# Moving the gate computation into attention, the row loads to the ScalarE queue, and narrowing the waits of late buffers

## The chip, the cores and the metric

The kernel runs on one core of one Trainium2 chip. The metric is the device time of one execution in microseconds, lower is better. Before the change the median of three runs is 730.36 us (727.07 to 731.42).

## What is computed

Attention within chunks of 64 positions, then a mixture of experts with one expert per token, chosen by cosine similarity. Everything is float32. Cut to what matters:

```python
# attention: q, k, v of shape (8, 8, 576, 64), in chunks of 64
scores = (q_c @ k_c.T) / sqrt(64)
attn = softmax(scores)                      # over the 64 keys of the chunk
x = (attn @ v_c)                            # -> (4608 tokens, 512)
# router and experts: 8 experts, w1 (8, 512, 1024), w2 (8, 1024, 512)
logits = (x / (|x| + 1e-6)) @ en.T / tau    # en: normalised expert embeddings
e = argmax(logits)
gate = 1 / (sum(exp(logits - max(logits))) + 1e-9)
out = gate * (relu(x @ w1[e]) @ w2[e])      # for each token with its own e
```

## The kernel before

**Two stages, one TensorE program.** Attention goes over 36 tiles `t` of 128 tokens. The expert stage goes over steps `j` (called blocks here): a block is 128 rows, 64 tokens of one expert in its lower half (`s` = 0) and 64 of another in its upper half (`s` = 1). One side works up from expert 0, the other down from expert 7. There are 37 blocks in this run; 36 of them are unrolled, and the last stands in a conditional section (`more`, L872). The schedule is manual: each engine runs its instructions in the order in which the Python code writes them.

**Attention** (L764 to L811). For a tile: transpose q and k (`turn_qk`), scores, subtract the maximum, Exp on ScalarE (`weights`), transpose, multiply with v (`values`), transpose x (`turn_x`), which also puts the sum of squares of each row beside it, then the eight logits. Four tiles make a group. For a group, `pick` (L514) finds the expert and `place` (L530) computes each token's row in a DRAM table `spots`, ordered by expert. `put` (L595) writes a tile's records there with an indirect DMA issued by GpSimd. A record is 512 values of x and 16 more: eight logits, the token number (`TOK`) and the sum of squares (`SQ`). Records wait in the ring `xr` of eight tiles; a slot is written again when its store has landed.

**Between the stages.** `groups`, `pad_places` and `places` (L646 on) turn the counts into tables: `src_row` (where a block's rows start), `eblk` (its expert) and `fresh` (whether the expert's weights have to be loaded). Padding records are stored last. Blocks 0, 1 and 2 hold rows of experts 0 and 7 alone, so they are loaded early (`load_early`), and the hidden layer of blocks 0 and 1 is computed in pieces inside attention (`early_parts`).

**Experts.** `load_x` (L144) reads two row numbers into registers and issues six DMAs, all on the SyncE queue: four pieces of x and two of the sixteen extra values (`spot`). `turn_xb` (L184) transposes the rows on VectorE. `hidden_part` (L213) does 64 matmuls for each half, then Relu on ScalarE and a transposition on VectorE. `result` (L242) does 64 matmuls, scales with the gate on ScalarE and writes out through an indirect DMA. `gates` (L196) computes the gate of a block: a square root on ScalarE, four VectorE operations, an Exp on ScalarE and two more VectorE operations. In the unrolled loop (L849) the hidden layer of block j+1 comes before the result of block j (of j-1 from the fourth round on), and the rows of block j+2 are transposed in the middle of hidden j+1.

**Weights.** Two buffers per layer and side. Buffer 0 is loaded in attention with experts 0 and 7. Buffer 1 is in the pool `late`, on bytes that attention used; block 4 (`LONE`) is the first to use it. `load_w` (L166) issues a load which moves nothing unless `fresh` is set. The first layer's weights of block 3 go out from ScalarE's queue, all later ones from SyncE's, in one order with the row loads. A weight load may go when the buffer's last reader is done: those of block j+2 wait for the matmuls of block j.

Of the kernel before, what the change touches and what calls it, by code (L numbers as in the profile page):

```python
# [9 lines left out]
FP32 = mybir.dt.float32  # L10
BF16 = mybir.dt.bfloat16
I32 = mybir.dt.int32
AF = mybir.ActivationFunctionType
ALU = mybir.AluOpType
AX = mybir.AxisListType
# [10 lines left out]
def kernel(  # L26
# [42 lines left out]

    MW = 16  # L70
    W = D + MW
    TOK, SQ = E, E + 1
    R = N + G * NE
    SPARE = E * R
    spots = nc.dram_tensor("spots", (SPARE + G, W), FP32, kind="Internal").ap()
# [47 lines left out]
            skip_runtime_bounds_check_because="a count of comparisons, less than this",  # L123
        )

    def load_rows(j, rows):

        xin[j] = xin_sb[j % XBUF]
        ins = []
        for s in range(2):  # L130
            for b in range(G // Q):
                c = s * (G // Q) + b
                ins.append(
                    nc.sync.dma_start(
                        out=xin[j][:, c * P : c * P + P],
                        in_=rows[s][Q * b : Q * b + Q, 0:D].rearrange("i (r d) -> r i d", d=P),
                    )
                )
            ins.append(
                nc.sync.dma_start(out=spot[G * s : G * s + G, j], in_=rows[s][:, D:W])  # L140
            )
        return ins

    def load_x(j):  # L144
        rows = []
        for s in range(2):
            row = number(src_row[G * s : G * s + 1, j - NE : j - NE + 1], SPARE, ENG.SP)
            rows.append(spots[ds(row, G), :])
        load_rows(j, rows)

    def first_rows(s, j, n):
        r0 = (0, E - 1)[s] * R + G * j
# [40 lines left out]
            )  # L193
        mo[j] = {"xT": xT}

    def gates(j):  # L196
        d = mo[j]
        lg = spot[:, j, 0:E]
        rn = bp.tile([P, 1], FP32, tag="rn", name="rn")
        lmax = bp.tile([P, 1], FP32, tag="lmax", name="lmax")  # L200
        sh = bp.tile([P, E], FP32, tag="sh", name="sh")
        gate = bp.tile([P, 1], FP32, tag="gate", name="gate", bufs=4)
        nc.scalar.activation(rn, spot[:, j, SQ : SQ + 1], AF.Sqrt)  # L203
        nc.vector.tensor_reduce(lmax, lg, axis=AX.X, op=ALU.max)
        nc.vector.tensor_scalar(rn, rn, 1e-6, None, ALU.add)
        nc.vector.reciprocal(rn, rn)
        nc.vector.tensor_scalar(sh, lg, lmax, rn, ALU.subtract, ALU.mult)  # L207
        nc.scalar.activation(sh, sh, AF.Exp, accum_out=gate)  # L208
        nc.vector.tensor_scalar(gate, gate, 1e-9, None, ALU.add)
        nc.vector.reciprocal(gate, gate)  # L210
        d["gate"] = gate

    def hidden_part(j, s, b, pool, tag, ps=None):  # L213


# [28 lines left out]
    def result(j, ps_y):  # L244
        d = mo.pop(j)
        ps = ps_y.tile([P, D], FP32, tag="y", name="y_ps")
        for c in range(KF):
            for r in range(P // Q):
                nc.tensor.matmul(  # L249
                    ps[Q * r : Q * r + Q],  # L250
                    lhsT=d["hT"][:, c, Q * r : Q * r + Q],
                    rhs=w2_sb[r // 2][buf_of(j)][:, c],
                    start=(c == 0),
                    stop=(c == KF - 1),
                )
        y = bp.tile([P, D], FP32, tag="y", name="y", bufs=3)
        nc.scalar.activation(y, ps, AF.Copy, scale=d["gate"])  # L257
        ins = nc.gpsimd.indirect_dma_start(  # L258
            out=out,
            out_offset=bass.IndirectOffsetOnAxis(ap=spot[:, j, TOK : TOK + 1].bitcast(I32), axis=0),  # L260
            in_=y,
            in_offset=None,
            bounds_check=N - 1,
            oob_is_err=False,
        )
        tc.declare_no_dep(ins.ins, group="rows", reason="blocks hold different tokens")
        tc.add_to_no_dep_group("rows", ins.ins)
# [8 lines left out]
    with (  # L276
# [26 lines left out]
        pref = one.tile([P, E], FP32, name="pref")  # L303
        e_base = one.tile([P, E], FP32, name="e_base")
        ones = one.tile([P, E], FP32, name="ones")
        part_i = one.tile([P, 1], I32, name="part_i")
        second = one.tile([P, 1], FP32, name="second")
        at = one.tile([P, 1], FP32, name="at")
# [18 lines left out]
        def constants():  # L327
# [5 lines left out]
            nc.gpsimd.memset(blank, 0.0)  # L333
            nc.gpsimd.memset(blank[:, D + TOK : D + TOK + 1].bitcast(I32), NO_ROW)
            nc.gpsimd.memset(ones, 1.0)
            nc.gpsimd.memset(before, 0.0)
            nc.gpsimd.memset(eqb_all[:, 0], 0.0)
            nc.gpsimd.memset(jump[:, 1], 1.0)
# [97 lines left out]
        def weights(t):  # L436
            a = st[t]["a"]
            nc.scalar.activation(a, a, AF.Exp, scale=scale)
# [75 lines left out]
        def pick(b):  # L514

            n, t = sizes[b], sum(sizes[:b])
            NE = [P, n, E]
            lg = copied.pop(b)
            lmax = wk.tile([P, RB], FP32, tag="lmax", name="lmax")[:, 0:n]
            sel = wk.tile([P, RB, E], FP32, tag="sel", name="sel")[:, 0:n]  # L520
            pm = wk.tile([P, RB], FP32, tag="pm", name="pm")[:, 0:n]
            nc.vector.tensor_reduce(lmax, lg, axis=AX.X, op=ALU.max)
            nc.vector.tensor_tensor(sel, lg, lmax.unsqueeze(2).to_broadcast(NE), ALU.is_equal)
            nc.vector.tensor_tensor(sel, sel, pref.unsqueeze(1).to_broadcast(NE), ALU.mult)
            nc.vector.tensor_reduce(pm, sel, axis=AX.X, op=ALU.max)
            nc.vector.tensor_tensor(
                eqb[:, t : t + n], sel, pm.unsqueeze(2).to_broadcast(NE), ALU.is_equal
            )

        def place(b):  # L530

# [232 lines left out]
        for t in range(-3, NT + 3):  # L764
# [29 lines left out]
                    load_v(b)  # L794
            if 0 <= t + 2 < NT:
                weights(t + 2)
            if t - 2 in ends:
                pick(ends[t - 2])
            if early_t <= t < early_t + NE:
# [14 lines left out]
        pad_places()  # L814
        put(len(to_put))
        places(0, 2)
        early_parts(NT + 3, 0)
        places(2, NST)
        nc.vector.tensor_copy(n_steps, mid[0:1])

    late_p = ctx.enter_context(tc.tile_pool(name="late", bufs=1))
    for s in range(2):
        w1_sb[s].append(late_p.tile([P, KD, F], FP32, name=f"w1_{s}1"))
    for s in range(2):
        w2_sb[s].append(late_p.tile([P, KF, D], FP32, name=f"w2_{s}1"))


    load_x(NE)
    load_x(NE + 1)
    load_w1(LONE)  # L830

    with (
        tc.tile_pool(name="ps_h", bufs=4, space=PSUM) as ps_h,
        tc.tile_pool(name="ps_y", bufs=2, space=PSUM) as ps_y,
    ):
        def hidden(j, turn=None):
            for s in range(2):
# [5 lines left out]
                    if turn + XBUF < NJ:  # L843
                        load_x(turn + XBUF)

        gates(0)

        LEAST = NT
        for j in range(LEAST + 1):  # L849
            if j == 0:  # L850
                gates(1)
            elif j + 1 < LEAST:
                hidden(j + 1, j + 2 if NE < j + 2 < LEAST else None)
                if NE <= next_of(j + 1) < NJ:
                    load_w1(next_of(j + 1))
            if j == 1:
                load_w2(LONE)
            if j + 2 < LEAST:
                if j + 2 <= NE:
                    turn_xb(j + 2)  # L860
                    load_x(j + 2 + XBUF)
                gates(j + 2)

            i = j if j < NE else j - 1
            if j != NE:
                result(i, ps_y)
                if NE <= next_of(i) < NJ:
                    load_w2(next_of(i))
# [3 lines left out]
        def more(j):  # L872
            with tc.If(steps > j - NE):
# [3 lines left out]
                hidden(j)  # L877
                if j + 2 < NJ:
                    load_w1(j + 2)
                gates(j)  # L880
                result(j, ps_y)
                if j + 2 < NJ:
                    load_w2(j + 2)
# [32 lines left out]
```

## Time and profile before

The profiled execution has a span of 735.0 us. The stages were read off the timeline of TensorE:

| stretch, us | what TensorE does |
|---|---|
| 0 to 206 | attention, and the hidden layer of blocks 0 and 1 between its tiles |
| 206 to 270 | blocks 0 to 5, with two holes |
| 270 to 709 | blocks in steady state, one step each 13.8 us |
| 709 to 726 | the last block, in the conditional section |
| 726 to 735 | the last store and the end of the program |

| group of instructions | busy, us | count |
|---|---|---|
| hidden matmuls, L229 | 279.9 | 4736 |
| result matmuls, L249 | 273.2 | 2368 |
| activation table loads, L203 and L208 | 47.5 each | 37 each |
| Relu, L238 | 44.2 | 74 |
| scaling of the result, L257 | 25.4 | 37 |
| transposition of rows, L188 | 43.1 | 74 |

A line of the timeline has the start, the duration, the engine, the line, the operation with what it writes and reads, and how many instructions were merged into it. In square brackets stands how long the engine was idle before it, and which engine, line or DMA ended that. For TensorE such a bracket is lost time; for the other engines idle time costs nothing by itself. `SPq` is the SyncE queue, where the duration is that of issuing a DMA and not of moving its data. A slice of the page is 18.4 us.

### The profile page before, as it was taken

The page shows a single profiled execution, that of the slowest core. Times are in us where ns is not written, and L with a number is a line of the kernel's source. Part 1 is how long each engine was busy: PE and PEld are TensorE (multiplying, and loading weights), DVE is VectorE, ACT ScalarE, POOL GpSimd, SP SyncE. Part 2 cuts the span into 40 slices and gives each one's busy share as a digit, 9 for nine tenths or more (in the row PEclk, how much of TensorE's full clock was granted, in tenths as well). Part 3 has the DMA queues.
Part 4 walks back from the last instruction along what each step waited for, and adds up shares of the span by engine and source line. Part 5 has one row for each costly group of instructions (what it writes and reads, how often), then busy time and mean ns, then how long its engine had stood idle before and what let it go on. Part 6 is the DMA issues. An engine that isn't in the chain of part 4 may idle for free. (4 is left out here: it accounts for less than half of the span.)

```text
span 735.0 us, 24771 instructions
## 1 busy us (share of the span) xinstructions
PE 685.2 (93%) x10327; PEld 399.4 (54%) x10327; DVE 264.0 (36%) x729; ACT 286.3 (39%) x518; POOL 123.9 (17%) x188
## 2 busy tenths in 40 slices
PE   6589999998969979999999999998999999999994
PEld 5579898986624434444444444443454554554441
DVE  4347787887272321321321321321122222222100
ACT  4346666664243333343343343342334334334112
POOL 7114454434131001001001001000000000000010
PEclk9779999998889999999999999999999999999998
DMA  9989999989727811116784416789751264411340
GB/s 197 191 193 212 250 246 253 242 198 327 285 82 275 276 29 56 35 42 207 254 324 170 162 44 222 275 314 330 270 180 43 72 234 159 147 45 44 132 169 16
DMA packets 139445, 132.36 MB, mean 180 GB/s; under 512 B 85332, under 2 KB 105812, under 8 KB 139328
## 3 DMA queue, kind: packets, MB, share of 16 engines
q1 hardware_dynamic: 130192, 101.95, 47.4%
q0 software_dynamic: 9104, 28.75, 12.7%
q8 instruction: 83, 1.36, 0.8%
q14 instruction: 34, 0.28, 0.1%
q10 hardware_dynamic: 32, 0.02, 0.0%
HBM read 349.52 MB, written 21.46 MB: 505 GB/s over the span
## 5 line engine op out<-in xcount | busy, mean ns | idle before, releaser
L229 PE MATMUL h_ps<-w,xbT 128*32 128x256 f32 x4736 | 279.9, 385 | 14.3 <-DMA w<-in_moe_w_dram 8.0
L249 PE MATMUL y_ps<-w,hT 128*32 128x512 f32 x2368 | 273.2, 592 | 4.6 <-DMA w<-in_moe_w_dram 3.2
L229 PEld LDWEIGHTS h_ps<-w,xbT 128*32 128x32 f32 x4736 | 167.5, 112 | 124.6 <-issue 32.8
L249 PEld LDWEIGHTS y_ps<-w,hT 128*32 128x32 f32 x2368 | 86.9, 110 | 161.3 <-issue 149.2
L239 DVE STREAM_TRANSPOSE hT<-h 128x512 f32<-128x512 f32 x74 | 52.6, 711 | 299.1 <-ACT h L238 299.1
L238 ACT ACTIVATE h<-h_ps 128x512 f32<-128x512 f32 x74 | 44.2, 597 | 217.7 <-PE h_ps L229 213.9
L258 POOL DMA_INDIRECT out_dram<-y,spot x37 | 36.3, 980 | 479.6 <-ACT y L257 426.7
L257 ACT ACTIVATE y<-y_ps,gate 128x512 f32<-128x512 f32 x37 | 25.4, 687 | 102.3 <-PE y_ps L249 102.3
L208 ACT ACT_TABLE_LOAD x37 | 47.5, 1283 | 24.6 <-DVE sh L207 24.5
L203 ACT ACT_TABLE_LOAD x37 | 47.5, 1283 | 2.8 <-DMA w<-in_moe_w_dram 2.2
L598 POOL DMA_INDIRECT spots<-xr,dest x36 | 37.1, 1031 | 48.9 <-DVE dest L563 16.1
L379 POOL DMA_DIRECT2D qx<-in_q_dram x40 | 35.1, 884 | 60.0 <-PE tr L402 59.5
L489 ACT COPY xT<-tr 128x512 f32<-128x512 f32 x36 | 21.1, 586 | 59.2 <-PE tr L487 59.2
L188 DVE STREAM_TRANSPOSE xbT<-xin 128x256 f32<-128x256 f32 x74 | 43.1, 621 | 0.1
L402 PE MATMUL tr<-ident,kx 128*128 128x128 f32 x144 | 24.6, 299 | 14.1 <-DMA kx<-in_k_dram 14.0
L499 PEld LDWEIGHTS rt_ps<-enT,xT 128*128 128x128 f32 x288 | 37.1, 202 | 1.0 <-issue 0.8
L499 PE MATMUL rt_ps<-enT,xT 128*128 128x8 f32 x288 | 36.6, 254 | 0.0
L407 DVE COPY qxT<-tr 128x512 f32<-128x512 f32 x36 | 24.8, 688 | 21.3 <-PE tr L402 20.5
L426 DVE TENSOR_REDUCE mx<-sc 128x8 f32<-128x512 f32 x36 | 24.9, 691 | 17.4 <-PE sc L418 16.4
L458 PE MATMUL pv<-v,aT 64*64 64x65 f32 x1152 | 27.5, 233 | 2.6 <-issue 2.2
L418 PE MATMUL sc<-kxT,qxT 64*64 64x64 f32 x1152 | 27.3, 235 | 0.4 <-issue 0.4
L458 PEld LDWEIGHTS pv<-v,aT 64*64 64x64 f32 x1152 | 21.9, 141 | 9.5 <-issue 9.0
(137 smaller groups left out, 446.4 us busy)
## 6 DMA issues: line engine op xcount, KB each, us to landing
w<-in_moe_w_dram SPq DMA_DIRECT2D x146, 2048.0 KB
xin<-spots SPq DMA_DIRECT2D x160, 64.0 KB
kx<-in_k_dram SPq DMA_DIRECT2D x32, 256.0 KB
qx<-in_q_dram POOLq DMA_DIRECT2D x32, 256.0 KB, 5.5
v<-in_v_dram SPq DMA_DIRECT2D x56, 144.0 KB
w<-in_moe_w_dram ACTq DMA_DIRECT2D x2, 2048.0 KB
spot<-spots SPq DMA_DIRECT2D x80, 4.0 KB
qx<-in_q_dram POOLq DMA_DIRECT2D x8, 128.0 KB, 6.7
```

The source lines that it names most:

```text
L188: nc.vector.transpose(xT[:, :, cols].rearrange("p c (b i) -> p b c i", i=Q), t[:, s * (D // 2) : (s + 1) * (D // 2)].rearrange("p (b i c) ...
L203: nc.scalar.activation(rn, spot[:, j, SQ : SQ + 1], AF.Sqrt)
L208: nc.scalar.activation(sh, sh, AF.Exp, accum_out=gate)
L229: nc.tensor.matmul(ps[Q * r : Q * r + Q, b].rearrange("p (k i) -> p k i", i=Q), lhsT=d["xT"][:, c, t0 : t0 + Q], rhs=w[:, c, r], start=(c ...
L238: nc.scalar.activation(h, ps, AF.Relu)
L239: nc.vector.transpose(hT[:, :, G * s : G * s + G].rearrange("p k (b i) -> p b k i", i=Q), h.rearrange("p b (k i) -> p b k i", i=Q),)
L249: nc.tensor.matmul(ps[Q * r : Q * r + Q], lhsT=d["hT"][:, c, Q * r : Q * r + Q], rhs=w2_sb[r // 2][buf_of(j)][:, c], start=(c == 0), stop= ...
L258: ins = nc.gpsimd.indirect_dma_start(out=out, out_offset=bass.IndirectOffsetOnAxis(ap=spot[:, j, TOK : TOK + 1].bitcast(I32), axis=0), in_ ...
L379: eng.dma_start(out=x[done : done + n], in_=src[b, :, s : s + n, :].rearrange("h p d -> p h d"),)
L458: nc.tensor.matmul(pv[CH * c : CH * c + CH, par, i], lhsT=d["aT"][r0 : r0 + CH, i, CH * c : CH * c + CH], rhs=v_t[b][r0 : r0 + CH, i, cb, ...
L499: nc.tensor.matmul(rt_ps[:, batch_of[t][0] % 2, batch_of[t][1]], lhsT=d["xT"][:, c], rhs=enT[:, c], start=(c == 0), stop=(c == KD - 1),)
L598: ins = nc.gpsimd.indirect_dma_start(out=spots, out_offset=bass.IndirectOffsetOnAxis(ap=at, axis=0), in_=m, in_offset=None, bounds_check=S ...
```

## The change

It has four parts. First, the gate is computed in attention, for a group of four tiles at once, and written into the record (field `GATE`), so that it arrives with the rows. The square root becomes a power of 0.5 on GpSimd, which spares ScalarE its change of tables. Second, the row loads of all blocks from 3 on are issued by ScalarE, so that only weights are left on SyncE. Third, the pools made after attention (`late`, `ps_h`, `ps_y`) wait only for those earlier users whose bytes they take over, and not for all users of the pools that lay there. Fourth, the order at the start of the expert stage: the rows of block 2 are transposed before the long tables of `places`, the weights of block 4 are asked for first, and the rows of block 5 are loaded ahead of the loop.

```diff
-    TOK, SQ = E, E + 1
+    TOK, SQ, GATE = E, E + 1, E + 2
...
-    def load_rows(j, rows):
+    def load_rows(j, rows, eng=nc.sync):
...
-                    nc.sync.dma_start(
+                    eng.dma_start(
...
-            row = number(src_row[G * s : G * s + 1, j - NE : j - NE + 1], SPARE, ENG.SP)
+            row = number(src_row[G * s : G * s + 1, j - NE : j - NE + 1], SPARE, ENG.Activation)
             rows.append(spots[ds(row, G), :])
-        load_rows(j, rows)
+        load_rows(j, rows, nc.scalar)
...
-    def gates(j):
-        d = mo[j]
-        lg = spot[:, j, 0:E]
...
-        nc.scalar.activation(rn, spot[:, j, SQ : SQ + 1], AF.Sqrt)
-        nc.vector.tensor_reduce(lmax, lg, axis=AX.X, op=ALU.max)
-        nc.vector.tensor_scalar(rn, rn, 1e-6, None, ALU.add)
-        nc.vector.reciprocal(rn, rn)
-        nc.vector.tensor_scalar(sh, lg, lmax, rn, ALU.subtract, ALU.mult)
-        nc.scalar.activation(sh, sh, AF.Exp, accum_out=gate)
-        nc.vector.tensor_scalar(gate, gate, 1e-9, None, ALU.add)
-        nc.vector.reciprocal(gate, gate)
-        d["gate"] = gate
...
-        nc.scalar.activation(y, ps, AF.Copy, scale=d["gate"])
+        nc.scalar.activation(y, ps, AF.Copy, scale=spot[:, j, GATE : GATE + 1])
...
+            sq = xr[:, t % NX : t % NX + n, D + SQ]
+            nc.gpsimd.tensor_tensor(rn, sq, halves[:, 0:n], ALU.pow)
+            nc.vector.tensor_scalar(rn, rn, 1e-6, None, ALU.add)
+            nc.vector.reciprocal(rn, rn)
+            nc.vector.tensor_tensor(sh, lg, lmax.unsqueeze(2).to_broadcast(NE), ALU.subtract)
+            nc.vector.tensor_tensor(sh, sh, rn.unsqueeze(2).to_broadcast(NE), ALU.mult)
...
+        def gates(b):
...
+            nc.scalar.activation(sh, sh, AF.Exp)
+            gs = wk.tile([P, RB], FP32, tag="gs", name="gs")[:, 0:n]
+            nc.vector.tensor_reduce(gs, sh, axis=AX.X, op=ALU.add)
+            nc.vector.tensor_scalar(gs, gs, 1e-9, None, ALU.add)
+            nc.vector.reciprocal(xr[:, t % NX : t % NX + n, D + GATE], gs)
...
                 weights(t + 2)
+            if t - 3 in ends:
+                gates(ends[t - 3])
             if t - 2 in ends:
                 pick(ends[t - 2])
...
         places(0, 2)
+        turn_xb(2)
         early_parts(NT + 3, 0)
         places(2, NST)
...
-    late_p = ctx.enter_context(tc.tile_pool(name="late", bufs=1))
+    late_p = ctx.enter_context(tc.tile_pool(name="late", bufs=1, reuse_waits="tile"))
...
+    load_w1(LONE)
     load_x(NE)
     load_x(NE + 1)
-    load_w1(LONE)
+    load_x(NE + 2)
...
-        tc.tile_pool(name="ps_h", bufs=4, space=PSUM) as ps_h,
-        tc.tile_pool(name="ps_y", bufs=2, space=PSUM) as ps_y,
+        tc.tile_pool(name="ps_h", bufs=4, space=PSUM, reuse_waits="tile") as ps_h,
+        tc.tile_pool(name="ps_y", bufs=2, space=PSUM, reuse_waits="tile") as ps_y,
...
-        gates(0)
...
-            if j == 0:
-                gates(1)
-            elif j + 1 < LEAST:
+            if 1 < j + 1 < LEAST:
                 hidden(j + 1, j + 2 if NE < j + 2 < LEAST else None)
...
-            if j + 2 < LEAST:
-                if j + 2 <= NE:
-                    turn_xb(j + 2)
-                    load_x(j + 2 + XBUF)
-                gates(j + 2)
+            if j + 2 == NE:
+                turn_xb(NE)
+                load_x(NE + XBUF)
```

## The prediction

> **What bounds the kernel now.** I read the page first. TensorE is busy 93% of the span, and the slices show it short of full in the attention part and again near slices 11 to 14 and 27. The chain that ended last holds only the final store, so I took the waits from the timeline of TensorE.
>
> ```profile
> PE 685.2 (93%) x10327; PEld 399.4 (54%) x10327; DVE 264.0 (36%) x729; ACT 286.3 (39%) x518; POOL 123.9 (17%) x188
> PE   6589999998969979999999999998999999999994
> L203 ACT ACT_TABLE_LOAD x37 | 47.5, 1283 | 2.8 <-DMA w<-in_moe_w_dram 2.2
> ```
>
> Next, the timeline of TensorE from 195 us (start, us, engine, line, what, count, idle before):
>
> ```profile
> 205.78 7.05 PE L249 MATMUL y_ps<-w,hT 128*32 128x512 f32 x64
> 218.49 9.50 PE L229 MATMUL h_ps<-w,xbT 128*32 128x256 f32 x128 [5.66 <-DVE xbT L188]
> 227.80 7.06 PE L249 MATMUL y_ps<-w,hT 128*32 128x512 f32 x64
> 234.66 7.09 PE L229 MATMUL h_ps<-w,xbT 128*32 128x256 f32 x128
> ...
> 261.24 8.61 PE L229 MATMUL h_ps<-w,xbT 128*32 128x256 f32 x128 [5.71 <-DMA w<-in_moe_w_dram]
> ...
> 508.02 7.06 PE L249 MATMUL y_ps<-w,hT 128*32 128x512 f32 x60 [3.17 <-DMA w<-in_moe_w_dram]
> 516.43 7.11 PE L229 MATMUL h_ps<-w,xbT 128*32 128x256 f32 x128 [1.35 <-DMA w<-in_moe_w_dram]
> ```
>
> A step is 128 matmuls of L229 (6.9 us from start to start) and 64 of L249 (6.9), 13.8 us. From 269.9 to 504.8 and from 516.5 to 709.2 TensorE is busy in every microsecond (the windows give 234.90 of 234.90 and 192.70 of 192.70), so work taken off other engines there is worth nothing. Only the holes can be won: 5.66, 5.71, 3.17 and 1.35 us, and the two slow stretches after the long ones: 9.50 and 8.61 instead of 7.09, 2.4 and 1.5 us. Sum 19.8 us.
>
> Who ends these holes? VectorE and ScalarE at the first, the SyncE queue at the second:
>
> ```profile
> 215.82 1.28 ACT L208 ACT_TABLE_LOAD   x1
> 217.63 0.16 DVE L210 RECIPROCAL gate<-gate 128x1 f32<-128x1 f32 x1
> 217.72 1.14 DVE L188 STREAM_TRANSPOSE xbT<-xin 128x256 f32<-128x256 f32 x2
> 225.39 1.95 SPq L169 DMA_DIRECT2D w<-in_moe_w_dram  x2
> 230.20 4.42 SPq L140 DMA_DIRECT2D spot<-spots  x1
> 261.01 3.95 SPq L169 DMA_DIRECT2D w<-in_moe_w_dram  x4
> ```
>
> Block 2's rows were long in SBUF; their transposition (217.72) stood on VectorE behind the gates of blocks 0 and 1, which waited for ScalarE's table loads. The second hole ends 0.23 us after SyncE issued the weights of block 5 (261.01): no expert changed, so nothing had to move, but the issue stood behind row loads slowed by the two weight loads of 225.39. At 487.53 likewise: that block's weights could go when its matmuls ended (476.4), but SyncE was issuing rows from 475.03 to 486.05.
>
> [...] 5.66 us idle, then granted clock 0.74 over 9.3 us; after 3.17 us none.
>
> **The change part by part.** *Gates out of the expert steps.* 74 table loads (95 us of ScalarE), and per block two activations and six VectorE operations go. In the full stretches this is hidden by TensorE. It counts at the first hole: with gates(0), gates(1) gone and turn_xb(2) before places(2,...), the transposition follows the `fresh` row at 208.6, before result(0) ends at 212.83. First hole and slow stretch go: block 2 starts at 212.8 instead of 218.5.
>
> *Gates into attention.* Per group of four tiles VectorE gets seven small operations of 0.15 to 0.20 us (rows L522 to L526), about 1.4 us; ScalarE one Exp of 0.2; GpSimd one power, unpriced by page or trace. Its nearest row, a 128x8 tensor_tensor, took 0.20 us; I allow 0.2 to 1.5. It is on the path where iota waits for stores (178.10) just when VectorE wants it. VectorE has no idle from 160.5 to 162.2 in such a group; x is written until 165.92 and transposed from 166.44, a slack of 0.5 us against 0.85 added ahead. So about 0.4 us in late groups, none in early ones (`before` takes 0.22 us there, 0.6 later). Also the first store of a group waits for its gate, some 2 us later; its slot is rewritten 7.3 us after issue (147.78 to 155.11) with 6.0 us to land, so 0.7 us may show. Lower end 0, upper end 8 groups of 1.4 = 11 us. I take 2.5.
>
> *Rows on the ScalarE queue.* The cost of one load there is not in the trace. On SyncE it is 4.4 us for six issues (213.43 to 217.85) and 5.9 from load to load; two weight issues of ScalarE took 1.43 us (229.30), 0.7 each; six of them and about 1 us for the two registers make 5.2. In a steady step ScalarE then has 5.2 + 1.9 (two Relu of 0.60, one y of 0.69) = 7.1 of 13.8 us. Relu of half 1 waits behind the issues, until about 12.6 us after the step's start; its hT is wanted 20.8 us after. Hidden. But at the start three loads (3, 4, 5) stand ahead of y(0) and Relu of block 2. They can't begin before the padding stores have landed (213.4): 213.4 + 3 x 5.2 - 0.8 = 228.2. Then y 0.69, two Relu, two hT of 0.71, half an xbT 0.6: block 3 starts at 231.8. TensorE ends result(1) at 226.6 and idles 5.2 us, then pays 2.4 us of slow clock: block 3 ends at 241.3, before 241.75. Nearly all of the first win is given back.
>
> *Weights alone on SyncE.* Block 4's weights go out near 210 instead of 225, its second half when load 4 has begun (about 222), and are there by 230, wanted at 248. Block 5's null load goes when block 3 ends (241.3). So the second hole (5.71) and its slow 1.5 go: result(3) starts at 241.3 + 3 x 6.9 = 262.0 instead of 269.66, 7.7 us earlier. At 476.4 the new weights go 11 us earlier; they and the second layer's are 8 MB, 21 us at the 373 to 401 GB/s that the windows from 490 to 505 show, wanted 27 us after the first issue; so both holes there (4.5 us) should close. In the built program a row load waits for the transfer eight before it on either queue; near a change of experts that is a weight of the step before, some 10 us old: a few us, inside the Relu's slack.
>
> *Waits by bytes.* Late buffers wait only for users of their own bytes. This concerns the second weight buffers, which lie on attention's tiles, and the PSUM banks. The expert number comes only at 208.4, so it lets the first half go near 210, counted above; no hole of before names a PSUM user of another bank, so the banks bring nothing.
>
> *Tail.* Block 36 has load 39 ahead of its Relus on ScalarE: 711.0 + 0.7 + 4.4 = 716.1, when Relu of half 1 is due at 717.2. 0 to 1 us; I take 0.3.
>
> Sum: +2.5 - 7.7 - 4.5 + 0.3 = -9.4; 730.4 - 9.4 = 721.0.
>
> **The rivals.** *Issue on ScalarE is slow while weights move* (chance 0.25). For: a row issue took 0.57 us at the median but up to 4.55 on SyncE, 4.42 at 230.20. Load 5 meets the weights of block 4; then block 3 starts 4.4 us later, half of the 4.5 stays, the tail takes 1: +2.5 - 3.3 - 2.2 + 1 = -2.0, 728. Against: those shared one queue with the weights. *VectorE becomes the bound of attention* (0.12): the full 11 us, with the slow issue and no gain at 508: +11 - 3.3 + 1 = +8.7, 739, slower. For: VectorE's full rows around each group. Against: it idles 0.76 us in each other tile. *ScalarE's loads don't delay block 3* (0.11): hole of 5.2 and slow 2.4 go too: 713.4. For: only if issues are near 0.3 us. Against: every issue shown is 0.5 or more.
>
> **How the numbers follow.** The forecast has 0.52. Its own unknowns (attention 0 to 5, the three loads 2 us either way) spread it over 716 to 725. The range is 713 to 733: it takes in the slow issue with its spread, and leaves out most of the VectorE case. One per cent is 7.3 us: faster needs under 723.1, most of the forecast (0.42), the last rival, and a little of the slow issue: 0.58. Within 1%: 0.30. Slower: 0.12.
>
> **What would show it.** Right: block 2's matmuls follow result(0) with no gap; a gap of about 5 us moves in front of block 3, ended by the transposition; none before block 5; none near 505; no table load after attention. Attention's last L229 ends 0 to 5 us later than 205.9. Wrong: Relu rows on ScalarE that wait so long that TensorE gaps recur in steps with weight traffic; row issues of over 1 us on ScalarE; or attention longer by over 5 us.

## The result and the profile after

The changed kernel takes 750.37 us at the median (747.58 to 752.08, four runs) against 729.5 us (727.07 to 731.42) for the kernel before: a ratio of 1.0284, 95% interval 1.0239 to 1.033. It is slower by almost 3%, where the prediction had it faster by 1.3%. A second measurement of both on another chip gave 752.55 (two runs) and 729.17 us, 1.0305 (1.02 to 1.0411). Medians and ratios count executions in the faster of two states; it matters for one run alone, the first with only the gates moved, where five of twelve executions, the traced one among them, were slower.

The page of the changed kernel first, the engine totals and TensorE's slices (here 18.7 us each):

```profile
PE 684.5 (92%) x10327; PEld 391.5 (52%) x10327; DVE 235.1 (31%) x570; ACT 174.1 (23%) x342; POOL 133.0 (18%) x198
PE   5589998999992999999989999987999999999994
```

ScalarE has lost 112 us of work and VectorE 29, as meant; no table load is left in the expert stage. TensorE does the same work, and, after attention, has a deep notch in slice 13 and shallow ones in slices 21, 27 and 28. Its timeline after attention (start, us, engine, line, operation, count, idle before) shows them; L212 is the hidden layer, L232 the result:

```profile
204.75 7.05 PE L232 MATMUL y_ps<-w,hT 128*32 128x512 f32 x64
211.62 7.09 PE L212 MATMUL h_ps<-w,xbT 128*32 128x256 f32 x128
218.53 7.05 PE L232 MATMUL y_ps<-w,hT 128*32 128x512 f32 x64
239.14 8.77 PE L212 MATMUL h_ps<-w,xbT 128*32 128x256 f32 x128 [13.56 <-DVE xbT L188]
...
254.60 13.99 PE L212 MATMUL h_ps<-w,xbT 128*32 128x256 f32 x256
268.42 7.04 PE L232 MATMUL y_ps<-w,hT 128*32 128x512 f32 x64
...
383.19 7.96 PE L232 MATMUL y_ps<-w,hT 128*32 128x512 f32 x58 [3.11 <-DMA w<-in_moe_w_dram]
...
498.71 8.66 PE L232 MATMUL y_ps<-w,hT 128*32 128x512 f32 x64 [2.73 <-DMA w<-in_moe_w_dram]
...
520.86 9.09 PE L232 MATMUL y_ps<-w,hT 128*32 128x512 f32 x58 [4.74 <-DMA w<-in_moe_w_dram]
```

The hole ahead of block 2 is gone (211.62 follows the result of block 0 directly), and so is the one ahead of block 5 (254.60 runs through two hidden layers). In their place stands one of 13.56 us ahead of block 3. In the steady part, where before had holes only near 510, there are now holes at 383, 499 and 521, each ended by a weight transfer and each followed by a stretch at the slow clock (granted at 0.52 from 383 to 386, at 0.50 from 499 to 501 and from 521 to 523).

What did the weights wait for? The waits of the SyncE queue from 205 us to the end (engine, line, what it waited for: us in total, times, longest), where L169 issues the weights:

```profile
SPq L169 <- DMA xin<-spots: 259.2, 59, 16.1
SPq L169 <- DMA w<-in_moe_w_dram: 87.7, 12, 10.5
SPq L169 <- PE y_ps L232: 25.3, 7, 7.7
```

SyncE issues nothing but weights now, and it spends 259 us waiting for the landing of row loads, which ScalarE issues. Before, its weights waited for TensorE to be done with a buffer, and for no row load:

```profile
SPq L134 <- DVE xbT L188: 86.7, 25, 4.7
SPq L169 <- PE y_ps L249: 28.6, 21, 5.6
```

No weight needs a row. The wait comes from the completion semaphores, as the trace's records of the transfers show, which name the semaphore that each one raises and those that it waits for. From 205 us on, SyncE (142) and ScalarE (224) issue 366 transfers. They raise the same eight semaphores, and 364 of them wait for the very one that they raise. GpSimd's 45 transfers raise eight others. A step of the changed kernel issues six row transfers and four weight loads; the last transfer on a weight's semaphore was a row load 73 times and another weight 70 times, and a row load had a weight ahead of it 70 times. The trace of before has eight semaphores for its 366 transfers as well, taken in turn (in 345 of 358 cases the same one comes again with the eighth transfer after it), but there 364 of the transfers stand in one queue, in that order, and the wait shows little (1.7 us of weights for weights). The Relus on ScalarE show the other direction, again from the table of waits:

```profile
ACT h L221 <- DMA spot<-spots: 90.6, 14, 9.2
ACT h L221 <- DMA w<-in_moe_w_dram: 67.4, 10, 11.2
ACT h L221 <- DMA xin<-spots: 57.4, 9, 8.3
```

A Relu needs neither. The row loads that stand ahead of it on ScalarE wait, and some of them for weights (67.4 us, in ten waits). So weights wait for rows, and rows for weights and for ScalarE's own work. In the issues of weights by SyncE from 490 to 506 us of the changed kernel (three windows of the timeline) the effect is seen: they go out one at a time until 500, just when the experts change. The two long waits in this stretch were ended by other weights (12.5 us together); ahead of the hole at 383 SyncE had waited 7.0 us for a row load.

```profile
491.99 0.09 SPq L169 DMA_DIRECT2D w<-in_moe_w_dram  x1
498.70 0.38 SPq L169 DMA_DIRECT2D w<-in_moe_w_dram  x1
500.29 2.85 SPq L169 DMA_DIRECT2D w<-in_moe_w_dram  x3
```

The kernel before had sent its four together:

```profile
487.53 4.06 SPq L169 DMA_DIRECT2D w<-in_moe_w_dram  x4
```

### The profile page after: what moved, and what is told of

Its sections match the earlier page's. It is cut to its first block, busy times and chain, and to the rows that moved or that the text cites. A ratio compares the mean times of both kernels' runs of the same rounds, so it can differ in the third digit from the quotient of the medians.

```text
span 748.1 us, 24343 instructions
## 1 busy us (share of the span) xinstructions
PE 684.5 (92%) x10327; PEld 391.5 (52%) x10327; DVE 235.1 (31%) x570; ACT 174.1 (23%) x342; POOL 133.0 (18%) x198
## 3 DMA queue, kind: packets, MB, share of 16 engines
q0 software_dynamic: 9104, 28.75, 12.5%
## 5 line engine op out<-in xcount | busy, mean ns | idle before, releaser
L212 PE MATMUL h_ps<-w,xbT 128*32 128x256 f32 x4736 | 283.3, 382 | 16.1 <-DVE xbT L188 13.6
L232 PE MATMUL y_ps<-w,hT 128*32 128x512 f32 x2368 | 283.9, 602 | 11.7 <-DMA w<-in_moe_w_dram 10.6
L212 PEld LDWEIGHTS h_ps<-w,xbT 128*32 128x32 f32 x4736 | 164.1, 110 | 128.5 <-issue 17.6
L232 PEld LDWEIGHTS y_ps<-w,hT 128*32 128x32 f32 x2368 | 89.3, 112 | 173.4 <-issue 157.9
L240 ACT ACTIVATE y<-y_ps,spot 128x512 f32<-128x512 f32 x37 | 25.4, 687 | 163.7 <-PE y_ps L232 114.4
L387 PEld LDWEIGHTS tr<-ident,kx 128*128 128x128 f32 x144 | 17.6, 149 | 22.5 <-issue 16.7
L387 PE MATMUL tr<-ident,qx 128*128 128x128 f32 x144 | 23.5, 290 | 2.4 <-DMA qx<-in_q_dram 2.4
```

Source lines behind the costliest of these rows:

```text
L212: nc.tensor.matmul(ps[Q * r : Q * r + Q, b].rearrange("p (k i) -> p k i", i=Q), lhsT=d["xT"][:, c, t0 : t0 + Q], rhs=w[:, c, r], start=(c ...
L232: nc.tensor.matmul(ps[Q * r : Q * r + Q], lhsT=d["hT"][:, c, Q * r : Q * r + Q], rhs=w2_sb[r // 2][buf_of(j)][:, c], start=(c == 0), stop= ...
L387: nc.tensor.transpose(ps[:, i], a[:, i * P : i * P + P], ident)
```

## The experiments

Runs of one comparison share a chip and its runs of the kernel before; ratios are to those. Theory 1 is the reading above. Its rival, theory 2: the loss lies in the gates in attention, the narrower waits or the new order.

### Rows moved between the queues, and each main part alone

*The changed kernel with rows back on SyncE* (here and below, the engine that reads the row numbers into registers is changed along with it):

```diff
-        load_rows(j, rows, nc.scalar)
+        load_rows(j, rows, nc.sync)
```

> The changed kernel with the row loads of blocks 3 to 36 back on the SyncE queue; gates in attention, order and waits by bytes stay. Theory 1 (rows on ScalarE are the cause: they stand behind Relus there, and weights on SyncE then wait for rows through the completion semaphores that both queues take in turn): no hole at 383, at most the 4.5 us of before near 510, block 3 not 13.6 us late. About 750 - 14 (weight holes) - up to 13 at the entry = 723 to 736. Theory 2 (gates in attention, waits by bytes or the new order cost the time): stays at 745 to 752.

Measured: 739.58 us, ratio 1.0095 (1.006 to 1.013). The hole at 383 is gone and one of 4.19 us is left at 511, like before's. The total misses the range, for two reasons: the hole ahead of block 5 came back at 7.97 us, and on this chip the last matmuls of block 1 crawled for 7 us (called the crawl below; last section).

*The same rows on GpSimd* (`nc.gpsimd` in that line):

> The changed kernel with the same row loads issued by GpSimd, which has its own completion semaphores and almost no work in the expert stage. Theory 1: the holes near 383, 499 and 521 go (some 14 us), and the hole ahead of block 3 shrinks from 13.6 us to at most 4, as no Relu stands behind a load: 715 to 728. Theory 2: 745 to 752, as on SyncE. If issuing through GpSimd is itself slow (several us for each of six), holes in steady steps of 13.8 us would return, each ended by the transposition of rows: over 735.

Measured: 727.42 us, ratio 0.9921 (0.9891 to 0.9951), although its trace has the crawl as well. After it TensorE has no hole of over half a microsecond until the conditional block at 709, and no weight on SyncE waits for a row. Again on a chip without the crawl:

> The changed kernel with rows on GpSimd once more, beside the two others. Its first run (727) had no hole in the steady part, but 7 us of single matmuls near 212 and a slow clock after it, some 9 us, which the kernel before and the changed one did not show on their chip. Without that: 715 to 720; if it belongs to this kernel: 725 to 730.

Measured: 714.15 us (709.42 to 717.76), ratio 0.980 (0.9757 to 0.9843). This is just under its range, and the fastest median of the study. TensorE's timeline of that run shows the entry:

```profile
220.46 7.12 PE L212 MATMUL h_ps<-w,xbT 128*32 128x256 f32 x128 [0.40 <-DVE xbT L188]
...
234.25 14.00 PE L212 MATMUL h_ps<-w,xbT 128*32 128x256 f32 x256
```

Block 3 waits 0.40 us in place of 13.56, and blocks 4 and 5 follow without a gap; up to 690 us no hole is longer. Nothing but the issuing engine of the rows differs from the changed kernel, and 36 us lie between the two medians. They are of two chips, but the ratios, 0.980 and 1.0284, lie as far apart.

*The kernel before with rows on ScalarE, nothing else:*

> The kernel before with one edit: the row loads of blocks 3 to 36 are issued by ScalarE. Theory 1: slower by 10 to 20 us (740 to 750), with holes in the steps with weight traffic near 383, 500 and 520 that are ended by DMA w, and waits of SyncE's weight issues (L169) for row loads of over 100 us in all. Theory 2: the same as before, 727 to 733, as the cost lies in the other parts.

Measured: 760.86 us, ratio 1.0375 (1.0308 to 1.0442), above the range. The holes of the steady part are there, some 12 us later than in the changed kernel, since this chip has the crawl and a hole of 18.08 us opens at the entry (here ahead of block 2). SyncE's waits name the same cause:

```profile
394.91 8.33 PE L249 MATMUL y_ps<-w,hT 128*32 128x512 f32 x58 [2.43 <-DMA w<-in_moe_w_dram]
...
532.81 9.40 PE L249 MATMUL y_ps<-w,hT 128*32 128x512 f32 x58 [4.33 <-DMA w<-in_moe_w_dram]
```

```profile
SPq L169 <- DMA xin<-spots: 230.4, 56, 13.6
```

So this one part alone costs about as much as the whole change, or more (the intervals of the two ratios overlap a little). Theory 2 is out as the main cause.

*The kernel before with the gates in attention, nothing else* (the diff of the gates as in the change, rows on SyncE, old order and waits), twice:

> The kernel before with one edit: the gates are computed in attention and travel in the records; rows stay on SyncE, the old order and the old waits stay. Theory 1: attention costs nothing, the first hole (5.66 us and 2.4 us of slow clock) shrinks as no table load stands ahead of block 2's transposition, the weight holes of before stay: 721 to 730. Theory 2: the gates cost time in attention, 735 to 750.

> The kernel before with the gates in attention and nothing else, once more, as its first run had the same 7 us of single matmuls. If that is not of this kernel: block 2 starts 0 to 6 us earlier than in before, the hole ahead of block 5 stays: 722 to 730. If it is: 734 to 740.

Measured: 736.81 us and ratio 1.0031 (0.9989 to 1.0072) the first time, on a chip with the crawl; 740.15 us and 1.0124 (1.0073 to 1.0174) the second time, without it. Both times lie where theory 2 had put them, and the second is above both of its own ranges. So the largest part of the change brings nothing by itself and may cost about 1%, and theory 1 was wrong to give it a gain; as a smaller cause, theory 2 is partly right. The trace of the second run, of one of its longest executions (744.15 us), shows why no gain came:

```profile
216.97 7.11 PE L212 MATMUL h_ps<-w,xbT 128*32 128x256 f32 x128 [0.73 <-DVE xbT L188]
...
266.50 9.53 PE L212 MATMUL h_ps<-w,xbT 128*32 128x256 f32 x128 [14.86 <-DMA w<-in_moe_w_dram]
```

The hole ahead of block 2 shrank from 5.66 to 0.73 us, and the one ahead of block 5 grew from 5.71 to 14.86. Block 5 starts 49.7 us after SyncE's first row load (216.79) here, and 47.8 us after it in before (213.43). That first load comes 11.1 us after the last half of block 1's hidden layer starts in both. The entry is bound by the SyncE queue, which works through its row loads until block 5's weights; what TensorE does meanwhile counts for nothing. The 5.66 us hole was slack.

### Semaphores or ScalarE's order?

Weights on GpSimd, rows still on ScalarE: the order on ScalarE stays, but the two no longer share semaphores, as GpSimd's transfers raise eight of their own (in both first traces).

```diff
-        eng, e_t = (nc.scalar, ENG.Activation) if first_layer else (nc.sync, ENG.SP)
+        eng, e_t = (nc.scalar, ENG.Activation) if first_layer else (nc.gpsimd, ENG.Pool)
```

> The changed kernel with rows still on ScalarE, but the weights from block 4 on issued by GpSimd, whose transfers have completion semaphores of their own. Theory 1a (the holes at 383, 499 and 521 come from the completion semaphores that SyncE's weights and ScalarE's rows take in turn): these holes go, the 13 us hole ahead of block 3 stays, as the loads still stand ahead of the Relus: about 750 - 14 = 734 to 740. Theory 1b (ScalarE's order of instructions alone makes rows, and with them everything, late): the holes stay as well, 745 to 752.

Measured: 728.44 us, ratio 0.9979 (0.9942 to 1.0015), some 24 us under the changed kernel on the same chip, and below theory 1a's range. From the start of block 3's result to the end it takes 459.6 us, against 480.9 in the changed kernel and 465.2 in the kernel before on this chip: the holes that before had near 505 are gone too, and theory 1a had not counted them. The hole ahead of block 3 stays (13.03 us, ended by the transposition of rows); in the steady part one of 0.36 us is left:

```profile
505.12 6.63 PE L232 MATMUL y_ps<-w,hT 128*32 128x512 f32 x58 [0.36 <-DMA w<-in_moe_w_dram]
```

The DMA engines show it in the window from 370 to 375 us, ahead of the hole at 383: DMA share and GB/s are the last two columns. The first line is of the changed kernel.

```profile
370.00:375.00 5.00, 5.00 (x80) 2.64 (x75) 0.71 (x1) 1.28 (x2) 0.97 (x1) 1.00 0.40 96
```

With the weights on GpSimd:

```profile
370.00:375.00 5.00, 5.00 (x72) 1.92 (x64) 0.63 (x1) 1.18 (x2) 0.00 (x0) 1.00 1.00 369
```

In this window of the changed kernel the engines were less than half busy while SyncE held weights back. A single window depends on where the step stands (this run has a share of 0.45 from 360 to 365); from 350 to 380 the two moved 231 and 260 GB/s.

Theory 1a holds for the steady holes: ScalarE's order is not enough to make them. The edit changes the engine that issues the weights as well as their semaphores; that the semaphores are the cause rests also on the records of the transfers and on the waits: here GpSimd's weights wait for other weights (95.9 us, 50 times) and never for a row, and no Relu stands behind a weight. All twenty traces agree. With rows on ScalarE and weights on SyncE (six) there is a hole of 2.4 to 3.3 us in the step at 383 to 395. With both on SyncE (five) the steady holes are only those between 500 and 517. With one of the two on GpSimd (nine) none is over 0.4 us between 280 us and the conditional block.

### The hole ahead of block 3

*Rows of blocks 4 and 5 issued after block 2's Relus:*

```diff
     load_x(NE)
-    load_x(NE + 1)
-    load_x(NE + 2)
...
                 turn_xb(NE)
+                load_x(NE + 1)
+                load_x(NE + 2)
                 load_x(NE + XBUF)
```

> The changed kernel with one move in the order: the rows of blocks 4 and 5 are issued after block 2's Relus instead of ahead of them; rows stay on ScalarE. If the hole of 13.56 us ahead of block 3 is the time that three row loads stand in front of block 2's Relus on ScalarE, it falls to 0 to 3 us and the slow clock after it goes (1.7 us), while the three holes of the steady part stay: 750 - 13 = 735 to 741. If the hole is the late arrival of block 3's own rows, it stays: 747 to 752.

Measured: 753.21 us, ratio 1.0288 (1.0196 to 1.0381). Neither expectation came. Block 3 starts without a hole (226.98), but 14.34 us open ahead of block 4:

```profile
233.88 7.05 PE L232 MATMUL y_ps<-w,hT 128*32 128x512 f32 x64
255.28 16.88 PE L212 MATMUL h_ps<-w,xbT 128*32 128x256 f32 x256 [14.34 <-issue]
```

The edit was too weak: with block 6's, three loads still follow one another on ScalarE, now ahead of the next y and the next Relu, which waits until 253.33. The hole moves with the loads and keeps its size, so it is the row loads on ScalarE that make it, wherever they stand.

*Rows on SyncE and weights on GpSimd*, which leaves ScalarE its arithmetic and the two weight issues of block 3 (both edits from above):

> The changed kernel with the row loads on SyncE and the weights from block 4 on issued by GpSimd: nothing but Relus and scaling is left on ScalarE, and rows and weights have separate completion semaphores. If the 13 us hole ahead of block 3 in the run with weights on GpSimd and rows on ScalarE comes from the row loads standing ahead of block 2's Relus on ScalarE, it goes, with 1.7 to 2.1 us of slow clock: 728.4 - 15 = 711 to 717. If it comes from the late landing of the padding stores or of block 3's rows, a hole of 5 to 13 us stays: 718 to 729.

*The kernel before with its weights on GpSimd, nothing else:*

> The kernel before with one edit: the weights from block 4 on are issued by GpSimd, rows stay on SyncE, gates stay in the expert steps. If the holes of before at 256 (5.7 us) and near 505 (4.5 us) come from weights and rows in one queue, both go, and only the 5.66 us hole of the table loads stays: 729 - 11 = 716 to 721. If they come from the bandwidth of the weights, nothing changes: 727 to 731.

Measured: 732.18 us, ratio 1.0043 (1.0007 to 1.0079), and 726.88 us, 0.9957 (0.9935 to 0.998). Both missed. In each the holes near 510 are gone, and a new one stands ahead of block 3: 17.39 and 9.98 us. The SyncE queue of the first, with its loads of block 3's rows, shows what it comes from:

```profile
210.32 1.44 SPq L134 DMA_DIRECT2D xin<-spots  x2
...
212.73 5.26 SPq L134 DMA_DIRECT2D xin<-spots  x2
```

GpSimd had issued all four weight loads of block 4 by 213.7, 8 MB, and the DMA engines were full until 230 (shares of 0.92 to 1.03 from 210 on). Two row issues then took 5.26 us in place of 1.3, and the rows that they loaded, the second half of block 3, could be transposed only at 237.84, 20 us after their issue. Block 3's weights, which ScalarE issues, came another 3 us later. So these two runs settle nothing about ScalarE's order: the weights, no longer held back, took the rows' time instead. With rows on GpSimd and weights on SyncE the same rows were issued from 211.83 to 215.8 and block 3 started at 220.46, with the engines as full (0.99 to 1.07 from 205 to 230). There GpSimd's 148 issues of x took 0.72 us each on the mean, and none of its pairs from 205 to 245 over 1.50 us. The longest single issue on SyncE took 4.55 us in before, and a pair 6.26 us in the first run here; on ScalarE the longest single one took 2.83 us in the changed kernel, and a pair 5.89 us with the weights on GpSimd. So rows on GpSimd gain two things, semaphores of their own and an issue that the weights do not stretch, and for this hole no run parts the two.

*Block 4's weights asked for last in the code, and the third part undone:*

```diff
-    load_w1(LONE)
     load_x(NE)
     load_x(NE + 1)
     load_x(NE + 2)
+    load_w1(LONE)
```

> The changed kernel with block 4's first-layer weights asked for after the row loads of blocks 3, 4 and 5 instead of ahead of them. If the row loads start late because the padding stores share the DMA engines with these weights, the first load starts about 9 us after result(0) does instead of 12, the hole ahead of block 3 shrinks from 13.6 to about 10 us, and the steady holes stay: 745 to 750. If the weights now come too late for block 4 (wanted some 9 us after block 3 starts), another hole takes that back: 750 to 756.

> The changed kernel without its third part: the pools made after attention wait for all users of the pools that lay there, as before. The prediction gave this part no value of its own except that block 4's weights may go near 210. Same time, 747 to 753. If the narrower waits matter, slower by several us.

Measured: 757.55 us, ratio 1.0339 (1.0269 to 1.041), and 757.15 us, 1.0347 (1.0257 to 1.0438), neither to be told from the 1.0284 and 1.0305 of the changed kernel. Both times are above their first ranges, on a chip with the crawl; the second would fit "slower by several us", but its ratio does not show that. The holes ahead of block 3 are only 3.86 and 5.43 us, since the crawl made TensorE some 9 us later and not the row loads; block 3 itself starts no earlier. The first edit did nothing, as SyncE has no row ahead of these weights: they went at 216.10, the rows at 222.01. Undoing the narrower waits, by removing `reuse_waits="tile"` in three places, did hold the weights back, to 222.60. The first row load then came 4.3 us after the last padding store was issued and not 7.1 as in the changed kernel; but the second load met the weights, two of its issues took 5.77 us, and the loads ended no earlier. So asking for the weights early costs the rows 2.8 us of start, and asking late costs it during the issue.

### What the parts are worth without the tangle

*The kernel before with rows on GpSimd, nothing else*, and *the changed kernel with rows on GpSimd and block 4's weights second:*

> The kernel before with one edit: the row loads from block 3 on are issued by GpSimd; gates stay in the expert steps, the old order and waits stay. The hole ahead of block 5 and the ones near 505 go (5.7 + 1.5 + 4.5 us), the 5.66 us hole of the gates ahead of block 2 and its slow clock stay: 729.5 - 11.7 = 715 to 721. [...]

> The changed kernel with rows on GpSimd, and block 4's weights asked for after the rows of block 3 instead of ahead of all rows. Rows of block 3 come some 3 us earlier, but there was no hole left to close there (0.40 us), and the weights, now on their own queue, don't stand behind rows in either case: the same as with rows on GpSimd, 709 to 718.

Measured: 720.62 us, ratio 0.9813 (0.9753 to 0.9872), inside its range, and 725.77 us, 0.9871 (0.9798 to 0.9944), above its range. Both are of a chip with the crawl, which costs the second more (last section). The holes near 256 and 510 are gone in both. Gates in attention, with the other parts, brought nothing on top of that.

*The kernel before with rows on GpSimd, and one transposition moved ahead of the tables*, beside the changed kernel with rows on GpSimd:

```diff
         places(0, 2)
+        turn_xb(2)
...
                 if j + 2 <= NE:
-                    turn_xb(j + 2)
+                    if j:
+                        turn_xb(j + 2)
```

> The kernel before with rows on GpSimd, and the transposition of block 2's rows ahead of the long tables of places, as in the changed kernel; the gates stay in the expert steps. If VectorE's order is what opens the 5.66 us hole ahead of block 2, the hole and its 2.4 us of slow clock go: 6 to 8 us under the kernel with rows on GpSimd alone (ratio 0.981), a ratio of 0.970 to 0.974. If the gates of blocks 0 and 1 keep ScalarE or VectorE busy so that Relu of block 2 is late, another hole opens: ratio 0.978 to 0.985.

> The changed kernel with rows on GpSimd, for comparison on the same chip. If the gates in attention cost about 4 us there, its ratio is 0.980 to 0.990 as in its two runs so far, some 5 us above the kernel that only moves the transposition. If they cost nothing: 0.970 to 0.976, the same as that one.

Measured: 716.51 us, ratio 0.9789 (0.9735 to 0.9843), and 726.07 us, 0.989 (0.9838 to 0.9941). The first has no hole ahead of block 2 (TensorE goes from the result of block 0 at once to block 2 at 211.35), so the gates need not leave the expert steps for that. Its ratio is that of the case in which another hole opens, though none did: its chip has the crawl, which costs it 6 us. It is not to be told from the 0.9813 without the moved transposition, so what the first hole is worth is not shown. It is 9.6 us faster than the version with gates in attention, whose ratio is in the case where the gates cost time. The two traces are 11.8 us apart; the crawl is some 3.5 us longer with the gates in attention, and attention 8.8 us. With rows on GpSimd the two best medians, 714.15 and 716.51 us, are of two chips and not to be told apart by their ratios.

### Both kernels once more

> The changed kernel itself, beside the others on the same chip: 747 to 752 with holes near 225, 383, 499 and 521. In four runs so far the last matmuls of block 1 in attention came one or two at a time for 7 us (205 to 212), which neither the kernel before nor the changed one had shown: if that belongs to those kernels it is absent here, if it belongs to the chip it appears here too.

> The kernel before itself, with a trace on the same chip: 729 to 735, holes near 213, 256 and 505. If the 7 us of single matmuls near 205 belong to the chip they appear here too, and if they belong to kernels with gates in attention they don't.

Measured: 752.55 and 728.08 us (the latter one run). The holes are in the expected places (14.60 us ahead of block 3, then 383, 499 and 521; before: 211, 253, 500), and neither trace has the crawl. As these two traces are of one chip, they are the better pair for the account below.

## Why the prediction was wrong

The prediction's sum, beside what the traces show. Attention is the start of the last half of block 1's hidden layer, entry the start of the result of block 3, less attention, and the steady part with the tail is the rest of the span:

| term | predicted, us | first pair of traces | pair on one chip |
|---|---|---|---|
| attention | +2.5 | -1.0 (202.30 to 201.27) | +3.8 (194.42 to 198.24) |
| entry | -7.7 | -0.2 (269.66 to 268.42, less -1.0) | +2.7 (261.11 to 267.62, less 3.8) |
| steady part and tail | -4.2 | +14.3 | +15.7 |
| span | -9.4 | +13.1 | +22.2 |

The trace of before shown with the prediction was of a long execution (736.7 us), which is why the first pair shows only 13 of the 21 us between the medians.

**The step that failed: "Weights alone on SyncE", and in it "a few us, inside the Relu's slack".** The prediction saw that transfers wait for the eighth before them on either queue (345 of 358 times in before), and priced one direction, a row that waits for an old weight. That came (67.4 us of Relus behind such rows, in ten waits). It left out the other: a weight that waits. On SyncE weights waited 259.2 us for rows and 87.7 us for other weights, where before it was none and 1.7. These rows stand on ScalarE behind Relus and scalings, and one load of a block, six transfers, takes six of the eight semaphores. So "at 476.4 the new weights go 11 us earlier" became weights that go out singly until 500, and where 4.5 us were to be won, the steady part with the tail lost 14 to 16. Where the queues were parted for the sake of independence, eight shared semaphores tied them together; the run with weights on GpSimd, which unties them, gave the steady part back (459.6 us in place of 480.9). The weight holes of before were also ascribed rightly: rows on GpSimd close them with the whole change (714 us) and without it (720.6).

**Mis-sized: the three loads ahead of block 2's Relus.** The mechanism was right: the gap in front of block 3, ended by the transposition, came. The term was "213.4 + 3 x 5.2 - 0.8 = 228.2" and measured 236.1. The loads started at 216.80, 7.1 us after the last padding store was issued (4.3 in the run that held block 4's weights back), and each took 6.4 us from load to load. Here are the first two and the y that stood behind them, ScalarE's timeline of the changed kernel:

```profile
216.80 1.92 ACTq L134 DMA_DIRECT2D xin<-spots  x2
...
223.40 1.76 ACTq L134 DMA_DIRECT2D xin<-spots  x2
...
236.07 0.69 ACT L240 ACTIVATE y<-y_ps,spot 128x512 f32<-128x512 f32 x1 [30.41 <-DMA xin<-spots]
```

Block 3 so starts at 239.14 and not 231.8, and the entry's 7.7 us are gone (-0.2 and +2.7 in the table). (What follows the loads was put at 3.6 us, though the terms listed there add up to 3.9; it took 3.1.) The rest of the entry was right: block 2 without a hole, no hole ahead of block 5.

**Wrong in the reading of before: the first hole as a win.** The 5.66 us ahead of block 2 were counted in under "Only the holes can be won". With gates alone that loss moved to the hole ahead of block 5, since the SyncE queue, and not TensorE, set when block 5 starts. A hole on the bounding engine is worth something only if nothing further on waits for another chain that is already running.

**Attention: the sign was right, the size uncertain.** The first pair showed no cost. Over the traces the last half of block 1's hidden layer starts at 194.4 to 202.3 us in six with gates in the expert steps (mean 198.0) and at 195.8 to 206.8 in thirteen with gates in attention (202.6; the first trace with the gates alone is left out). That is 4.6 us more, with a scatter of over 3 us in each set, inside the bounds of 0 and 11 that were given. The difference is -1.0 us in the first pair, and on the five later chips 1.7, 3.8, 6.8, 7.9 and 8.8. GpSimd's power, "unpriced by page or trace", took 1.05 us (L519, nine times), inside its 0.2 to 1.5.

**The rivals.** Slow issue on ScalarE did occur: the pair of row issues at 243.00 took 4.84 us while weights moved. The prediction set against it that the slow issues of before "shared one queue with the weights". This trace has issues on ScalarE stretched nearly as much as those on SyncE had been (4.84 us for two, and 4.94 for two at 242.04 of before), so a queue apart from the weights did not protect the issue. But that rival ended at 728, and no case had weights that become later than before. VectorE as the bound of attention, at 739, is neither shown nor ruled out as the reason why attention grew; it grew by less than the 11 us of that case. What was listed as a sign of error, "gaps recur in steps with weight traffic", is just what came; it had been written down without a time, so the range ended at 733.

Still open: why row issues on SyncE and ScalarE stretch while weights move and those on GpSimd do not (0.72 us on the mean), and what in attention the gates lengthen. A version of the changed kernel with more completion semaphores was not tried.

## What to carry to other kernels

When a transfer moves to another issuing engine, follow its completion semaphore in the built program in both directions: who waits for it, and whom it now waits for, since two queues with one set of semaphores were one queue with two fronts here (259.2 us of weights that waited for rows, 67.4 us of Relus behind weights). Look first for an engine with semaphores of its own and little to do; here rows on GpSimd gave 1.9% (1.3 to 2.5) without any other part of the change. And before a hole is counted as a win, ask which queue has been running since before it and will end the next one.

## What was not expected of the hardware

On three of the five later chips, in kernels of either kind, TensorE crawled through the last matmuls of block 1 just as attention ends. From the timeline of the changed kernel with rows on SyncE:

```profile
201.75 4.15 PE L212 MATMUL h_ps<-w,xbT 128*32 128x256 f32 x57 [0.78 <-ACT h L221]
206.76 0.64 PE L212 MATMUL h_ps<-w,xbT 128*32 128x256 f32 x3 [0.86 <-issue]
208.21 0.51 PE L212 MATMUL h_ps<-w,xbT 128*32 128x256 f32 x1 [0.81 <-issue]
...
212.48 8.41 PE L232 MATMUL y_ps<-w,hT 128*32 128x512 f32 x64
```

One to three matmuls go every 1.4 us for 7 us, "issue" means that nothing in the profile holds them, and the clock, granted at 0.50 from 210 to 215, makes the next 64 matmuls 1.4 us longer (up to 3 us in other traces). By the start of block 2 this costs 9 to 10 us with gates in attention, and 6 in the kernel with gates in the expert steps that has no hole there. On the two other chips no trace has it, of eight. What makes it is not known. The DMA records hold one hint: in the first traces of both kernels, which have no crawl, a transfer of the queue that the page lists as q8 starts 4.21 us (before) and 3.65 us (changed) after this last half does, and from 196 to 216 us the changed kernel's q8 moved 2 packets, where in each of two traces with the crawl (rows on SyncE; gates alone) it moved 1. Whether this is a cause or a consequence no run shows. The crawl is why ratios, and not times, are compared across chips above, and a ratio does not correct it fully: the kernel before, whose entry waits for its queue anyway, loses only some 3 us on these chips by its medians (733.3, 732.0 and 733.1 against 729.2 and 729.8; no trace of it was taken there).

Smaller: the prediction took the slow clock to follow only the long holes, since before had 0.74 over the 9.3 us after a hole of 5.66 us, and 1.00 from 508 to 515, after one of 3.17. In the changed kernel a hole of 2.73 us (498.71) was followed by 64 matmuls in 8.66 us in place of 7.04. The clock granted from 499 to 501 was 0.50. In the run without the third part a hole of 3.29 us (389.49) was not followed by a slow stretch (58 matmuls in 6.63 us, against 7.96 after the changed kernel's hole of 3.11 us). So the length of a hole alone does not decide, and each of the three weight holes was dearer than its length.
